# Another written-down order for the 5752 operations of a sparse-attention and two-layer mixture kernel

## The chip, the cores and the metric

The kernel runs on one core of a Trainium2 chip. The metric is the device time of one execution in microseconds; smaller is better. The time of the kernel before is the median of three runs.

## What is computed

Three stages follow each other (4 batches, 8 heads, 576 rows, head size 64; 2304 tokens of width 512; 8 experts with 1024 hidden units):

```python
scores = scale * np.matmul(q, k.transpose(0, 1, 3, 2))
kth = np.partition(scores, -32, axis=-1)[..., -32:-31]
scores = np.where(scores >= kth, scores, -1e9)          # the 32 largest of each row
attn = softmax(scores);  x = attn @ v                   # tokens, 8 heads side by side
logits = x @ w_gate + modality_bias[modality_id]
e = argmax(logits);  g = softmax(logits)[e]
x = g * (relu(x @ w1[e]) @ w2[e])                       # one expert for each token
h = x @ w_in;  solu = h * softmax(h)
out = layernorm(solu) * g_ln @ w_out
```

## The kernel before

**Attention.** The rows of a batch are cut into five tiles (four of 128 rows and one of 64). For each tile and pair of heads PE makes the scores (`pS`, L628). ACT copies them into `ss` (L649, L659), and DVE finds the 32nd largest value of each row: a maximum and a minimum of the two halves (L661, L662), then rounds of MAX8 and MATCH_REPLACE8 (L665 to L678). POOL and ACT make the masked exponentials `e` (L689 to L693). PE transposes them (L722, L733) and multiplies with the values (`po`, L755). ACT copies that into `oT` (L762), and one more matmul, `px` (L765), waits for the copy and gives the tile's rows and gate logits.

**Routing.** When the four pairs of a tile are done, its tokens are routed: DVE, POOL, ACT and PE work out the expert and the place of each token in that expert's list (the last step on DVE is L853, which adds to the count `cq`), and POOL scatters the rows into a list in DRAM (L858).

**First expert layer.** 14 slots of 128 tokens (`PLAN`) and a last, larger one take tokens from the lists. A slot may be taken when a given number of tokens is routed: 256 for slot 0, 384 for slot 1 and so on. POOL and DVE pick the fullest expert (L908, L915, L794 to L920), POOL gathers its rows from DRAM (`xg`, L933), PE transposes them (L960), DVE copies the result (`xT`, L966), and PE multiplies (`ph`, L1025; ACT makes `hh`, L1030; `py`, L1046). SP loads the expert's weights. The last slot uses fp32r matmuls of 448 columns (L1326, L1346) on split weights.

**Second layer.** Each group of 128 finished tokens goes through `moe2`: 24 matmuls of 512 columns into `u` in two halves (`ph`, L1067; ACT copy L1071; DVE maximum L1073, L1076; POOL L1077), exponentials on ACT (L1082), their product on DVE (L1084), the sums on POOL (L1090 to L1097), then two turns. A turn is four PE transposes of a half of `u` (L960), an ACT copy into the high part `lT` (L964), a DVE subtraction into the low part `lT` (L968) and 12 matmuls into `po` (L1128; the weights are `wo`). At the end ACT scales (L1137) and POOL scatters to the output (L1139).

Before all that, both second-layer weights are prepared from 64-bit floats (`statics`, L383 to L470) among the first attention tiles.

**The order.** The work is written as generators, called threads here (one for each unit of attention, pair, route, slot, group of tokens and so on). Each yields operations for one engine, or waits for buffers and events. At build time `Order.run` lists the threads that have an operation ready, and a digit of the table `ORDER` (base 36) says which one goes next:

```python
ready = [t for t in self.threads if t["op"] is not None]
...
if self.order is not None:
    th = ready[int(next(self.order), 36)]
...
op = th["op"]
op.fn()
```

So the table alone sets the sequence in which each engine's instructions stand, and which buffer each tile gets. Every engine runs its instructions in that sequence and waits where an operand isn't there yet. The costs that stand beside the operations are not used where a table is given, other than for bookkeeping.

Of the kernel before, what the change touches and what calls it, by code (L numbers as in the profile page):

```python
# [36 lines left out]
       "w": 4.587, "prep": -3.306, "ffn": 1.734, "front": -0.797, "static": -2.917, "const": -1.332}  # L37

ORDER = (
    "0022556001111111222202334444441115555513333554455556663666440000011233434366666667777555622223377703344441"  # L40
    "1225663226045437747747406244166644451000031111111130400000411333300033442121332155132333044345113544003002"
    "2221556420644464341444401111133622511114446463624461162233636556444412225115552666643315111111814443333332"
    "6675575751944228611434436633667114411111133011114445411122543323522224400445222255336065046005555110432222"
    "2200005561700205223616333333302660022221146007728584472226901553333384557744446661633334115665656213333547"
    "6222677788111425113316778122311145366676522233011100660001230005544112222222225113501133400555600511222467"
    "3311111115525444000113230000230550034434441111111000520002222113355555667335733302112446666553550000388877"
    "7617999894446361111118002455511220050005777444710005350053344992201187472242665111145333133311461114466115"
    "5115688888823662244166661743233223355443434343345352234452222622116010011224443304678776434234311224005511"
    "1112234343320335500044435553226610055671534444521053153536744154224526332222112002244003335255333000002344"
    "4611751160131557833333323436522245334775677676271166114492534763247788222283226233334623225577777766445443"  # L50
    "3666661226222757564126542524655772333043333115055353400042255000400223323000000011154021200042224004443456"
    "78822224811334555258570007301637788822662aa887800653347844785761334521604111100225562266644123333000046551"
    "1160011662242344552772060044034011120001112242112466666601177777665654522756565558856765888403033331133223"
    "2013232224445501133365533446553366001828333378835558803335454572201322621224411111455666163322412221154577"
    "2331301122305533334240113355541224551111110231200332456700543432224677757747418776662661777741365774422545"
    "3313436111022000133232455000111133335689842321434337422667533115511377122222254506411333453666112222245613"
    "4461556663347250132886868954424444442445663316666561111556111777745110433226565116231234002005555554331311"
    "1111144443152244533545545774201000122335444461551111322205300233400001331200134332400002211167880000544440"
    "2427351115453300000001022686622222474748807877112328664441140343345527704500442522666600077826558868990114"
    "5950411555700007556555034220222004455116665771581118882882223444445502266665773225100011111165335455522506"  # L60
    "0000022153231232311333466661102224255664134221115544432422233033555517757000102667788655522111115544127774"
    "4552311111000555777772944664304707225241115866282735311441434334455599033554aa445519a555775589633ab9255989"
    "8266400511166711167353011115001948882555007420344773333115766565576778945636776785157012334799993388942145"
    "5457443333233324656311022244222344003422300400011116614544336115844113393225957556641110500022272554440024"
    "6776225666200117734300100044846781711665333316744411411300172722999a64466977177763333311177859a11b11113354"
    "4488558188991116626227000555142553677677622264405245663362222554223633302220456666661145451111220885772655"
    "8776340846a91446767567755555552711111334455551288544122467133233035536531424250111111333465541100533222511"
    "4456063121332337891884545413355555254454622233622224775663557223337751130511689377454333512442266171455411"
    "22222005550000007654445577722802633725588a2bb01668888748717457559a6699973334556674445997a339a9aa9991155333"
    "3888888955674444555116877179444424541118167111304331221134434344555602344894331312334433455015556651566666"  # L70
    "4522222222215454666342111000231114444006006612301344220011661111104266726634311111311232555464113342884855"
    "56a430115881a811776533122252666645657528311899555583331332831466899998811188bb3377871178787111974553999799"
    "a91572722244469999a66333388544b559966136794444014367676226356566539181115555114377311117222992542433555446"
    "46467464647161333728111116633552223322776655645415111656578444017658744a9999132222244255568343322224445544"
    "47783333557672222111731223588667544224623389a6a886aa222755227898865534441111158944492557702264676387377765"
    "6558882993336646444064177166767014583376444499555779551878553555577a80999566673444628833333a69997aa4579944"
    "49778b8999925533a4444433000775507777755996663377433008341aaa1898805772434700003444356634444477760677800000"
    "2247744221111155566763333400200246611442200433333304001114110043400046631203446344644522115624545662226666"
    "656110441486697aa8779978873a444466448a22995588644409145801115701112700000441004661145511221333211222233332"
    "3351125555644025473222245733642236363677225453332272067751116575578888792222542422252078871668451133748666"  # L80
    "643345454564001544446000000333333565004460055788866777000706228389a965552336111155534113432351144302240556"
    "3333773331503400047776618902040655650053448827176368007883375345061111112224555444110344347227311111634322"
    "4306236676446386678344347572211666112244555677177845336655542222233554545318882456555824778355366623333356"
    "6255711422234462226760005006620400004754617322330072426665522222288226625000007464115566654005400040677666"
    "5787428000302221224453541110100223413344678777767711232222263450333555699772283455000000114356722355564343"
    "6011133711133322277111166661133266333366264511454545446222222266651444661342755227777733009586117344005451"
    "1332200000043345120522112216133114465667720221100411422222244553500012553232321243443445225331000000006767"
    "7734455454433554967757932233302271336655454666222788111133573454472215556660266699445323363332077472441314"
    "4455221113006622233600002364000023322246656557342220036433166222212000055005402004322444133233334230031300"
    "3330022222220002222202311121222341442220000000000221144000022110000000234444333333311331222533007700476666"  # L90
    "6666666444453455223333333111333323221115101111444223332202002200000111221100001111122324341132220022240002"
    "2444000000100133435523005004422121113345122111101230041443344030021100000000000000000000000000000011220000"
    "2221100001111111111111222222222230222331100022221113400300001222221100000002110000000000000011111000000001"
    "1111122033221000000000000000"
)
UNITS = 4
NEG = -3.0e38
# [1572 lines left out]
```

## Time and profile before

| | |
|---|---|
| median of 3 runs | 955.14 us (952.91 to 955.68) |
| profiled execution, its own time | 952.62 us |
| its span, first to last instruction | 950.8 us |
| PE busy | 874.6 us, 92% |
| DVE busy | 779.7 us, 82% |
| ACT busy | 670.9 us, 71% |
| POOL busy | 585.1 us, 62% |
| mean granted TensorE clock | 0.972 of full speed |

The span is 1.8 us shorter than the execution's own time. PE counts as busy while a matmul runs; PEld is its weight loads, which run beside matmuls. The windows view, quoted below, gives each engine's busy time in stretches of the span.

### The profile page before, as it was taken

To read this page: it belongs to the slowest core of one execution; us is meant where nothing else is said; L and a number is where in the kernel's file an instruction comes from. 1 tells how busy PE (TensorE), PEld (TensorE's weight loads), DVE (VectorE), ACT (ScalarE), POOL (GpSimd) and SP (SyncE) were. 2 spreads that over 40 slices of the span, in tenths; PEclk is the share of its full clock that TensorE was granted. 3 is DMA by queue.
4 is the path that set the end of the run, shared out by engine and by line. 5 is a ranking of instruction groups with operands and counts; after the bars stand their busy time and mean duration, and the time that the engine had idled before them with its cause. 6 is when DMAs were issued, how large, how long until landed. Compare 5 with 4: busy or idle time off the path is not lost.

```text
span 950.8 us, 21544 instructions
## 1 busy us (share of the span) xinstructions
PE 874.6 (92%) x6830; PEld 730.7 (77%) x6830; DVE 779.7 (82%) x2444; ACT 670.9 (71%) x1698; POOL 585.1 (62%) x1352
## 2 busy tenths in 40 slices
PE   5766787989999999999999999999999999999994
PEld 3544455977888888879888888888887988889872
DVE  7998998999999999999999999999999943422320
ACT  3867876878787778878877788788778863633432
POOL 4677856657666767675677677666677666520222
PEclk9888887999999999999999999999999999999998
DMA  6624233444624343455243434443432337624000
GB/s 173 188 67 138 91 89 93 124 115 140 174 79 148 112 137 113 119 157 154 79 137 103 125 90 138 121 123 113 136 96 86 114 107 224 195 89 118 6 23 26
DMA packets 140952, 110.72 MB, mean 116 GB/s; under 512 B 47233, under 2 KB 116893, under 8 KB 140830
## 3 DMA queue, kind: packets, MB, share of 16 engines
q1 hardware_dynamic: 136478, 93.92, 34.4%
q0 software_dynamic: 4352, 15.34, 4.7%
q8 instruction: 56, 0.92, 0.4%
q14 instruction: 66, 0.54, 0.2%
HBM read 97.11 MB, written 12.13 MB: 115 GB/s over the span
## 4 chain that ended last, share of the span: by engine, by line
PE 50%; DVE 14%; POOL 10%; ACT 5%; issue 5%; DMA 2%; POOLq 0%; DVEq 0%; ACTq 0%
PE po L1128 7%; PE ph L1025 7%; PE py L1046 7%; PE ph L1067 6%; PE po L755 5%; PE pS L628 4%; PE pt L722 4%; DVE M L669 3%; POOL e L691 2%; PE py L1346 2%; PE ph L1326 2%; DVE tht L678 2%; DMA xg<-xlist,li 2%; PE pt L960 1%; PE px L765 1%
## 5 line engine op out<-in xcount | busy, mean ns | idle before, releaser
L691 POOL TENSOR_TENSOR e<-ss,e 128x576 f32<-128x576 f32 x144 | 206.3, 1434 | 55.4 <-ACT e L690 52.9
L693 ACT ACTIVATE e<-e,nb 128x576 f32<-128x576 f32 x144 | 112.0, 778 | 25.7 <-POOL e L691 24.7
L669 DVE MATCH_REPLACE8 M<-tops,M 128x288 f32<-128x288 f32 x288 | 127.4, 445 | 0.0
L1025 PE MATMUL ph<-xT,wraw 128*128 128x128 f32 x960 | 126.2, 278 | 1.1 <-DVE M L662 0.5
L1046 PE MATMUL py<-hh,wraw 128*128 128x128 f32 x960 | 125.8, 278 | 1.1 <-ACT hh L1030 1.1
L690 ACT ACTIVATE e<-ss,bt 128x576 f32<-128x576 f32 x144 | 111.5, 778 | 19.4 <-POOL bt L689 19.2
L1025 PEld LDWEIGHTS ph<-xT,wraw 128*128 128x128 f32 x960 | 115.4, 192 | 6.3 <-issue 3.1
L1046 PEld LDWEIGHTS py<-hh,wraw 128*128 128x128 f32 x960 | 115.3, 192 | 5.6 <-issue 2.7
L1128 PE MATMUL po<-wo,lT 128*128 128x512 f32 x432 | 112.0, 404 | 2.6 <-ACT lT L964 2.6
L1067 PE MATMUL ph<-wi,yT 128*128 128x512 f32 x432 | 110.2, 403 | 0.8 <-ACT ss L649 0.7
L755 PE MATMUL po<-eT,vt 128*64 128x128 f32 (+1 forms) x1600 | 104.7, 273 | 5.2 <-DVE qT L533 1.9
L678 DVE MAX8 tht<-M 128x8 f32<-128x576 f32 x144 | 108.1, 754 | 1.2
L628 PE MATMUL pS<-kT,qT 64*128 64x288 f32 (+1 forms) x864 | 94.4, 322 | 10.0 <-DVE xs L776 4.3
L755 PEld LDWEIGHTS po<-eT,vt 128*64 128x64 f32 x1600 | 84.6, 140 | 20.7 <-ACT eT L725 5.8
L1128 PEld LDWEIGHTS po<-wo,lT 128*128 128x128 f32 x432 | 77.6, 188 | 23.8 <-DVE lT L968 3.3
L1067 PEld LDWEIGHTS ph<-wi,yT 128*128 128x128 f32 x432 | 78.3, 188 | 19.8 <-issue 1.6
L628 PEld LDWEIGHTS pS<-kT,qT 64*128 64x128 f32 (+1 forms) x864 | 72.2, 193 | 27.0 <-issue 7.8
L725 ACT ACTIVATE eT<-pt 128x512 f32<-128x512 f32 x144 | 82.0, 597 | 10.4 <-PE pt L722 9.8
L722 PE MATMUL pt<-identr,e 128*128 128x128 f32 x576 | 85.0, 284 | 4.1 <-ACT e L693 1.7
L722 PEld LDWEIGHTS pt<-identr,e 128*128 128x128 f32 x576 | 68.8, 146 | 12.7 <-ACT e L693 3.5
L661 DVE TENSOR_TENSOR M<-pS,ss 128x288 f32<-128x288 f32 x144 | 64.7, 450 | 9.3 <-ACT ss L659 7.2
L689 POOL TENSOR_SCALAR bt<-tht 128x1 f32<-128x1 f32 x144 | 34.0, 236 | 62.2 <-DVE tht L678 51.7
(256 smaller groups left out, 1848.4 us busy)
## 6 DMA issues: line engine op xcount, KB each, us to landing
wraw<-in_moe_w_dram SPq DMA_DIRECT2D x256, 256.0 KB
kr<-in_k_dram SPq DMA_DIRECT2D x32, 128.0 KB
qr<-in_q_dram SPq DMA_DIRECT2D x16, 256.0 KB
raw<-in_moe_w_out_dram SPq DMA_DIRECT2D x8, 512.0 KB
vt<-in_v_dram SPq DMA_DIRECT2D x32, 128.0 KB
raw<-in_moe_w_in_dram SPq DMA_DIRECT2D x8, 512.0 KB
wstage<-da SPq DMA_DIRECT2D x8, 256.0 KB
wc<-wstage SPq DMA_DIRECT2D x8, 256.0 KB
```

The costliest lines, as they stand in the source:

```text
L628: nc.tensor.matmul(bank[s][hf], x[r, a, p, :], kt[r, c, at:at + HALF], start=i == 0, stop=i == 2)
L669: nc.vector.match_replace(out=M, in_to_replace=rounds[r], in_values=M, imm_value=NEG)
L678: t0 = yield Op("DVE", 660, lambda: nc.vector.max(th, W), deps=[t0, tm])
L690: yield Op("ACT", 667, lambda: nc.scalar.activation(e, ss, AF.Relu, bias=bt, scale=-BIG))
L691: yield Op("POOL", 1360, lambda: nc.gpsimd.tensor_tensor(e, ss, e, op=OP.subtract))
L693: yield Op("ACT", 760, lambda: nc.scalar.activation(e, e, AF.Exp, bias=nb, scale=0.125, accum_out=z))
L722: nc.tensor.transpose(pt[:, c, :], ef[:, at:at + 128], ident)
L755: nc.tensor.matmul(po[hs, :n], w, x, start=c == 0, stop=c == 4)
L1025: nc.tensor.matmul(ph[:, :n], w[:, kk * 128:(kk + 1) * 128], x[0][:, kk, :n], start=kk == 0, stop=kk == KD - 1)
L1046: nc.tensor.matmul(py[c // k_][:, c % k_, :], w[:, c * 128:(c + 1) * 128], hs[m], start=m == 0 and c % k_ == 0, stop=m == KF - 1 and c % k ...
L1067: nc.tensor.matmul(ph, y[a][:, kk, :], wi[b][:, kk, i * 512:(i + 1) * 512], start=kk == 0 and j == 0, stop=kk == KD - 1 and j == 2)
L1128: nc.tensor.matmul(po, l[a][:, c, :], wo[b][:, kk, :], start=kk == 0 and j == 0, stop=kk == KF - 1 and j == 2)
```

## The change

Only the table `ORDER` is another one. Both tables have 5752 digits; the first 11 are the same, and 4864 of all differ. The operations, their shapes, the buffers' numbers and the plan of slots are the same.

```diff
 ORDER = (
-    "0022556001111111222202334444341111115555513333554455556663666440000011233434366666667777555622223377703344441"
...
+    "0022556001101111220112334441144455551445446666556657427747773222333327775335888447777436655355541288886662"
...
 )
```

**The last matmuls on PE.** Two groups of tokens are the last to go through the second layer. Here `po_14028` and `po_14112` are their results before, `po_14017` and `po_14090` after; `po_13894` is the result of the group ahead of them. A row of `L960` with `u` is a turn's transposes. Before:

```order
L1067 MATMUL ph<-wi_98,yT 128x512
L960 MATMUL pt<-identr,u 128x128 x4
L1128 MATMUL po_14028<-wo_100,lT 128x512
...
L960 MATMUL pt<-identr,u 128x128 x8
L1128 MATMUL po_14028<-wo_100,lT 128x512
...
L1128 MATMUL po_14112<-wo_100,lT 128x512
...
L960 MATMUL pt<-identr,u 128x128 x4
L1128 MATMUL po_14112<-wo_100,lT 128x512
```

Now:

```order
L1128 MATMUL po_13894<-wo_100,lT 128x512
...
L960 MATMUL pt<-identr,u 128x128 x4
L1128 MATMUL po_13894<-wo_101,lT 128x512
...
L1128 MATMUL po_14017<-wo_100,lT 128x512
...
L960 MATMUL pt<-identr,u 128x128 x8
L1128 MATMUL po_14090<-wo_100,lT 128x512
...
L960 MATMUL pt<-identr,u 128x128 x4
L1128 MATMUL po_14017<-wo_100,lT 128x512
...
L1128 MATMUL po_14090<-wo_100,lT 128x512
```

Behind the last L1067 stand 48 matmuls of L1128 before, and 60 now: 12 of the group ahead moved behind it, six on either side of the first turn's transposes. The two last groups now take turns, so that between the last transposes and the matmuls which read them stand 12 of the other group.

**The second route on DVE.** These are DVE's rows around the last step of the second tile's routing (L853) up to the pick's first step (L915); the other rows are attention units, the weights' low parts (`wo`) and the low parts of `qT`. Before:

```order
L669 MATCH_REPLACE M<-tops,M 128x288
L851 TENSOR_TENSOR rk<-pc,cq 128x8
L852 SCALAR_TENSOR_TENSOR rk,pos<-rk,oh 128x8
L853 TENSOR_TENSOR cq<-cq,pc 128x8
L665 MAX tops<-M 128x8
L672 MAX tops<-M 128x8
L669 MATCH_REPLACE M<-tops,M 128x288
L470 TENSOR_TENSOR wo_101<-pw,wo_100 128x512 x2
```

Now:

```order
L470 TENSOR_TENSOR wo_101<-pw,wo_100 128x512
L669 MATCH_REPLACE M<-tops,M 128x288
L533 TENSOR_TENSOR qT<-pt,qT 64x4x64
L851 TENSOR_TENSOR rk<-pc,cq 128x8
L852 SCALAR_TENSOR_TENSOR rk,pos<-rk,oh 128x8
L853 TENSOR_TENSOR cq<-cq,pc 128x8
L672 MAX abt<-M 128x8
L533 TENSOR_TENSOR qT<-pt,qT 64x4x64
```

DVE now has 299 instructions up to and with this L853 in place of 293, and in both orders 338 up to and with the first copy of gathered rows (L966). So 39 stand from the route to the copy in place of 45.

## Rows read from the trace of the kernel before

**Rows 1.** The page's part 1: busy time, share of the span, instructions.

```profile
PE 874.6 (92%) x6830; PEld 730.7 (77%) x6830; DVE 779.7 (82%) x2444; ACT 670.9 (71%) x1698; POOL 585.1 (62%) x1352
```

**Rows 2.** Windows: us, then busy time of each engine, granted clock, DMA share, GB/s.

```profile
0.00:10.00 10.00, 4.41 (x22) 3.20 (x22) 4.25 (x17) 3.66 (x8) 1.96 (x15) 1.00 0.45 96
10.00:165.00 155.00, 114.15 (x620) 71.92 (x622) 144.91 (x394) 110.53 (x259) 109.39 (x164) 0.86 0.41 123
165.00:200.00 35.00, 34.45 (x323) 31.83 (x322) 34.73 (x117) 28.27 (x78) 22.86 (x55) 1.00 0.42 123
200.00:750.00 550.00, 537.30 (x4710) 465.50 (x4709) 523.72 (x1710) 439.04 (x1149) 372.29 (x915) 1.00 0.42 122
750.00:900.00 150.00, 148.40 (x1004) 131.18 (x1003) 61.02 (x187) 73.54 (x182) 64.02 (x168) 1.00 0.40 123
900.00:950.80 50.80, 35.84 (x159) 27.10 (x157) 11.06 (x23) 15.86 (x29) 14.57 (x38) 0.91 0.06 23
```

**Rows 3.** PE's timeline at the end: start, us, instructions, idle before and its releaser.

```profile
915.35 5.75 PE L1067 MATMUL ph<-wi,yT 128*128 128x512 f32 x24
921.85 0.66 PE L960 MATMUL pt<-identr,u 128*128 128x128 f32 x4 [0.75 <-DVE u L1084]
923.20 3.32 PE L1128 MATMUL po<-wo,lT 128*128 128x512 f32 x12 [0.69 <-ACT lT L964]
926.36 1.03 PE L960 MATMUL pt<-identr,u 128*128 128x128 f32 x8
928.60 6.13 PE L1128 MATMUL po<-wo,lT 128*128 128x512 f32 x24 [1.21 <-ACT lT L964]
934.56 0.60 PE L960 MATMUL pt<-identr,u 128*128 128x128 f32 x4
935.85 3.33 PE L1128 MATMUL po<-wo,lT 128*128 128x512 f32 x12 [0.69 <-ACT lT L964]
```

**Rows 4.** Timelines of ACT and DVE in the same stretch.

```profile
918.34 0.60 ACT L1071 ACTIVATE u<-ph 128x512 f32<-128x512 f32 x1 [1.54 <-PE ph L1067]
921.10 0.69 DVE L1084 SCALAR_TENSOR_TENSOR u<-u,ex 128x512 f32<-128x512 f32 x1 [1.25 <-ACT ex L1082]
939.30 0.69 ACT L1137 ACTIVATE ot<-po,hrs 128x512 f32<-128x512 f32 x1 [3.50 <-PE po L1128]
```

**Rows 5.** Whom PE waited for, from 10 to 165 us: total, times, longest.

```profile
PE px L765 <- ACT oT L762: 6.8, 3, 3.6
```

**Rows 6.** DVE's groups, 10 to 165 us: busy, mean ns, idle before, releaser.

```profile
L661 DVE TENSOR_TENSOR M<-pS,ss 128x288 f32<-128x288 f32 x26 | 11.7, 449 | 4.0 <-ACT ss L659 3.6
```

**Rows 7.** Timelines of DVE, POOL and PE from the second route to slot 0.

```profile
146.97 0.15 DVE L853 TENSOR_TENSOR cq<-cq,pc 128x8 f32<-128x8 f32 x1
158.62 1.10 POOL L933 DMA_INDIRECT xg<-xlist,li  x1 [0.29 <-POOL li L929]
164.28 0.63 PE L960 MATMUL pt<-identr,xg 128*128 128x128 f32 x4 [0.18 <-DMA xg<-xlist,li]
165.34 0.68 DVE L966 COPY xT<-pt 128x512 f32<-128x512 f32 x1
```

**Rows 8.** The tile `xg`, all gathers: landing after issue, and who waited for it.

```profile
DMA to landing us min/median/max: 3.5/4.5/6.3
DVE xT L966: 2.4, 2
```

**Rows 9.** Whom PE waited for, 200 to 905 us: total, times, longest; the longest row.

```profile
PE px L765 <- ACT oT L762: 2.6, 4, 1.4
```

More of the change, by code (lines that the diff above doesn't have):

```diff
@@ L45 @@
[L45 to L54, printed above, removed]
@@ new lines @@
+    "2233223377544545420880112434236636663555662111122220111115455512445515551511211444454422222112223333666113"
+    "3677784664844663352111111114453311466771167444662422235434533444363637777333312222234322221144466551518833"
+    "4435355339777288224444113324677688511211211155334446665565666222372233333113333445655777771161168722024833"
+    "364422764382847945557586992411222555222a4488333989442aa292277444a33335563351353366887025343333211555467771"
+    "8331873333226226676888853113114444112222551114666566788437777221214222352111138335117133335562222688137331"
@@ new lines @@
+    "1122666223222222235112441111112255451611114334444444133111111666656a147372244aa3a3677774455556119427135517"
+    "7761261369999787111173632227776224251111133888171113445356658591113713163122241322220112222243111364111555"
+    "5111156776334777754544116666657333522253254343442133244452226222233441611554545451145762678742523411524162"
+    "22222225514322324455555555133155404551451162351344434336201166666773113222204472226565568117772222027a6644"
+    "2266464472211535668637322022222226234211516656511613540701811001175772221192999991335336676626241121334343"
@@ new lines @@
+    "3422555576337144457752056556777776215277441122834266512111342551133443434111111321155111222312444312444689"
+    "aa2333029166334862388066005582200012aaa0777bb8998934541622627600052200011131722264677550113332300005665771"
+    "1170031302720170043355600466411520041444300222668822888899999882484113267676788595956678666666925441122656"
+    "5651777834222574441772263345689181074232222220673604122673357761573325887774644455712263522222222664541341"
+    "1045414324420011144552254555514660021440013400000024234556745440055522115552561878733155684688777751336544"
@@ new lines @@
+    "5522223362222205541140343146455552226111731022557441213374221168484911556614642265506443433375366777121111"
+    "533706773363254599899a689548155555524459476611342216655611177671835511677634226577117786311153888645222222"
+    "7771222233662545456605571436222443151232342444666511500012000440000313112111343433671170010055667322114331"
+    "1363465555221111455220630073322228265511576466723111112603666353357006664700007700729944477777833a66688289"
+    "0116a1119187115166734448376675373887777333833a122456647838833266776765567837833468512131331225837225554312"
@@ new lines @@
+    "8011202544504355355302277788226646344878976772222222331099482615452333043334466610030778151121467633320077"
+    "7000003700555555666111661615657776300662449983332347756264545456668999a3033745564541133688784444699aa84781"
+    "032284813361447676111114611868841110100915546644444488129878a77899896b7579467a8877122553999aaa892258444708"
+    "45444333333126634452122553347773116433316611142222885344366112995522833b4477366622211544112322285673558511"
+    "63633737112288887452220221166555562278855073355536111711460111aaa452289a88582123aabb498999aa40330330244496"
@@ new lines @@
+    "98a64001988a5511614744832110155578828474643998754087785533446633633226233620666666462231777177220776267884"
+    "4348446940178787878666666789785261511884412377779974664537725512274646464677447367776122451172444562222213"
+    "1225568816667421477776565657112322146554253325466222246225776345520223257717554223777754662253345563333342"
+    "08227851115111066114456608000077777211265627589aa0155a9966185556667493355689994533444744444588337798996998"
+    "9851155767678885588894411941545584422333663336222111153353114113354553652834547778223455456331677727777565"
@@ new lines @@
+    "6333332333365646666778722224111551122442551771134552423112222222373773354445892288777722222238444b37757527"
+    "ab77771115325aa5888892472231118378838808794946466522988328482414663899988881121442997265651165651133344116"
+    "25777777786746966a45579aaaabb744668747454442554918847833367676035669999777a1255115344931111222228868296353"
+    "6456464664377311855255511552222122111534347766266115653678722465657752222544666256533011449352448433326467"
+    "451573334457577162222533112266885272433689aa89956555222267679222788887393312242222131816766333478877775650"
@@ new lines @@
+    "254477757875753aa788328807553a91455826333388036733305422224263315653368888365557247333357722222599889634b3"
+    "999222558789bb000755877333333888377088255558366a43333994660019a9a80733440000030444335664438744337766777000"
+    "0042211138885555116166111333510000220511666221454444161157703633333464111166666576335782446651621173633625"
+    "5053446016577644449359a50446757776133336643346637332783311557544440066650074330000436626667722774665543442"
+    "2503433847777455277131111115662255346424336225643377205677116614589777888262222277163111006667334665755462"
@@ L95 @@
+    "6666663333316334755001553444444435000551172233366222010204331133333302222220000111002222322322320033300246"
+    "6611100011101103345522100222311131231112233443311102001000332222333002000000000001000000000000002330002223"
+    "3222222330223314334443221143333221122452400220110000000000303011112210003301101111111111112222201110021120"
+    "1111110302211110022110100000"
 )
```

55 lines of the change are left out of this document (10 added, 45 removed).

## Prediction

> **What bounds the kernel now.** I read the busy shares first, then the stretches, then the timeline of the end, and last the place where the first expert slot starts. PE is busy 92% of the span and DVE 82% [rows 1], but these are averages over stretches with different limits [rows 2]. From 10 to 165 us DVE is busy 144.91 of 155.00 us and PE only 114.15: there is no expert work yet, so attention on DVE sets the pace, and DVE's 10.1 us of idle time are what an order could win there. From 200 to 750 us PE is busy 537.30 of 550.00 us and DVE 523.72, and from 750 to 900 us PE 148.40 of 150.00. So behind slot 0's start PE is the bound, with 12.7 and 1.6 us of idle time in those two stretches. In the last 50.80 us PE works 35.84 us: there it waits on its own last results.
>
> The end is the plainest part [rows 3]. The last L1067 is over at 915.35 + 5.75 = 921.10 us and the last L1128 at 935.85 + 3.33 = 939.18, so this tail takes 18.08 us. The work in it is 48 matmuls of L1128 at 5.75 / 24 = 0.240 us (the row of 24 back to back) = 11.5 us, and 16 transposes in 0.60 + 1.03 + 0.60 = 2.2 us: 13.7 us. The other 4.35 us are gaps: each turn's transposes or matmuls wait for DVE or ACT with nothing put between, and the first L1128 of a turn run stretched (3.32 us for 12 in place of 2.88) while the low part is still being made.
>
> **The change, part by part.** It adds and removes no instruction: DVE has 338 up to the first gathered copy in both orders, and the diff touches the table alone. So busy time should stay, and all that can change is who waits.
>
> *The tail.* Behind the last L1067 stand 60 matmuls now: 60 x 0.240 = 14.4 us, with transposes 16.6. Which gaps stay? The first group's second half of L1067 now ends 12 matmuls (2.88 us) before the last L1067 does. From the ACT copy of such a half to the transposes of its turn took 921.85 - 918.34 = 3.5 us [rows 3, 4], so those are ready some 0.7 us after the last L1067, and six matmuls of the group ahead (1.4 us) stand in that place: covered. Its eviction (the 0.69 us gap and the stretched start, together about 1.1 us) is covered by the other six. The eight transposes in the middle evict with nothing but the second four between: I leave half of 1.1 us there, 0.6, where the row before shows 1.21 because ACT was busy. The last turn is covered by 12 matmuls of the other group. So the tail is 16.6 + 0.6 = 17.2 us, and it holds 12 matmuls (2.88 us) that stood ahead before, where PE had no gap: the gain is 18.08 + 2.88 - 17.2 = 3.8 us. Bounds: 4.35 if no gap stays; 2.6 if the middle gap stays whole (1.21 + 0.5). What comes after PE, from the ACT scale at 939.30 us to the span's end, 11.5 us [rows 4], is the same.
>
> *Up to slot 0.* In these 155 us PE stood 6.8 us in three waits of `px` for the ACT copy `oT` [rows 5]. Behind `px` in PE's order stand the next scores, and DVE's L661, which needs their copy, sat idle 4.0 us [rows 6]. Counting PE's instructions between a pair's last `po` and its `px`: of the ten pairs ahead of the first expert matmul, three had none before (the first, fourth and tenth), and one has none now (the seventh); the second to fourth now have 12 or 13. So I expect about half of L661's 4.0 us back, 2.0 us. Bounds: all of DVE's 10.1 us, and a loss from the gather below.
>
> *The gather of slot 0.* From the second route to the copy of slot 0's rows DVE took 165.34 - 146.97 = 18.4 us for 45 instructions, 0.41 us each, and PE's wait for the rows was 0.18 us [rows 7], so the gather was just hidden. Now 39 instructions stand there: 6 x 0.41 = 2.5 us less cover. Behind the waiting copy the whole attention on DVE is queued, and behind PE's transposes the next `po`. But the six instructions are not lost, they stand ahead of the route, and POOL's list between scatter and gather (L858 to L933) is as long as before. I take no loss: the route's own steps (L851 to L853) had idle time in front of them which now has work in it. Bound: 2.5 us.
>
> *The middle.* Other waits of PE are short and many; the longest, `px` for `oT`, is 2.6 us in four waits [rows 9]. Of the 70 pairs behind the first ten, `px` directly behind its `po` stands twice before and twice now. I take 0; bounds are a gain of all 14.3 us of PE's idle time, and a loss from later slots: the DVE instructions from route to copy fall from 48 to 44 at slot 1, 50 to 45 at slot 5 and 55 to 47 at slot 6, and rise or stay within three at slots 2, 3, 4 and 7. At 0.41 us those are 1.6, 2.0 and 3.3 us of cover.
>
> *Sum.* 3.8 + 2.0 = 5.8 us. The profiled execution (952.62) would take 946.8; it lies 2.5 us under the median of 955.14. Against the median: 955.14 - 5.8 = **949.3 us**.
>
> **Rivals.**
>
> A. *The middle closes up too.* If the new order spares half of the middle's 14.3 us (7.1), the time is 949.3 - 7.1 = 942.2. For it speaks that DVE has 26.3 us of idle time from 200 to 750 us, so it could follow; against it, that the waits there are scattered and the counts above don't change. Chance 0.14.
>
> B. *The gather of slot 0 shows.* The head's 2.0 us don't come and 2.5 us of stall come in their place: 955.14 - 3.8 + 2.5 = 953.8, within the measurement. For it: only 0.18 us of slack in the rows; against it, as argued, that DVE's queue ahead has more work in it. Chance 0.17.
>
> C. *Slower: several gathers are uncovered.* Slots 0, 1, 5 and 6 lost 2.5, 1.6, 2.0 and 3.3 us of cover, 9.4 us together. A stall at L966 holds every attention unit behind it, and the later routes with them. If all show and only the tail's 3.8 us come back: 955.14 - 3.8 + 9.4 = 960.7. It decides for slower once 6.7 us show (3.8 plus 0.3% of the time). Against it: in all 14 gathers L966 waited 2.4 us on two occasions only [rows 8], and gathers land 3.5 to 6.3 us after issue, so most had slack. Chance 0.10.
>
> D. *PE isn't full in the middle.* The matmul row says 537.30 of 550.00 us, the weight-load row 465.50 [rows 2]. If the 537 were waits drawn out as work, DVE would be the next limit and its 26.3 us could go: 949.3 - 26.3 = 923.0. By the row of 24 matmuls in 5.75 us, which had no idle time before it and none inside, I hold PE's busy time for real work and give this 0.02. The Trainium skill ("Perfetto Trace Analysis", Identifying the Most-Contended Engine) says that matmul busy share is no good measure of how near TensorE is to its limit, and that the share of weight loads is; by that rule the middle would have 15% in hand. No run here shows that yet.
>
> That the table is the same program in effect isn't a rival: 4864 digits differ, and the sequences of all five engines do.
>
> **How the numbers follow.** The forecast has 0.57; its own range, from the tail's and head's bounds, is 945 to 952.5. Runs of this kernel scatter by about 0.3% (2.9 us), which I take as what can be told from no change: faster means under 952.3. The forecast is there with nearly all its chance; with A and D that is 0.69 after a little for the forecast's upper edge. Same, B and that edge: 0.19. Slower, C and a smaller share of B with worse luck: 0.12. The range of 8 in 10 reaches from A's 942 down to 941.5, and up to 957, part of the way to C.
>
> **What would show it.** *Right:* the stretch from the last L1067 to the last L1128 is about 17.2 us long with 60 matmuls, and L1128 waits for `lT` at most once there; `px` waits for `oT` less than 4 us in the head; slot 0's copy L966 starts near 163 us; PE's busy time stays within 3 us of 874.6. *Wrong:* L966 or L960 waits for gathered rows by over 2 us at slots 0, 1, 5 or 6; slot 0 starts after 165.3 us; PE's idle time from 200 to 900 us differs from 14.3 us by more than 4.

## The result and the profile after

| | before | changed |
|---|---|---|
| median of the runs | 955.0 us (952.91 to 955.68, 4 runs) | 941.82 us (940.89 to 944.39, 4 runs) |
| ratio | | 0.987 [0.9845, 0.9895] |
| profiled execution, its own time | 952.62 us | 944.39 us |
| its span | 950.8 us | 942.5 us |

The change makes the kernel faster by 13.2 us. The forecast was a gain of 5.8 us, so more than half of what came isn't in its sum. The profiled execution of the changed kernel is the longest of its four; another profiled one (below, the full change again) took 941.35 us.

Busy times of the changed kernel, as [rows 1]:

```profile
PE 874.3 (93%) x6830; PEld 729.7 (77%) x6830; DVE 773.9 (82%) x2444; ACT 670.3 (71%) x1698; POOL 582.4 (62%) x1352
```

PE's busy time is the same to 0.3 us in these two profiles (874.6 before; the changed kernel's second profile has 870.7). So nearly all of the time between the two comes out of waits. Where, the windows of the changed kernel tell, beside [rows 2]:

```profile
0.00:10.00 10.00, 4.41 (x22) 3.19 (x22) 4.17 (x17) 3.63 (x8) 1.96 (x15) 1.00 0.45 99
10.00:165.00 155.00, 115.86 (x613) 71.02 (x614) 143.73 (x391) 109.22 (x255) 108.01 (x160) 0.83 0.41 121
165.00:200.00 35.00, 35.00 (x323) 32.15 (x322) 33.50 (x116) 27.05 (x76) 21.96 (x55) 0.98 0.47 136
200.00:750.00 550.00, 540.49 (x4738) 467.67 (x4738) 524.46 (x1724) 444.90 (x1163) 375.60 (x921) 1.00 0.42 122
750.00:900.00 150.00, 148.85 (x1010) 132.33 (x1005) 59.09 (x179) 71.79 (x175) 63.71 (x174) 1.00 0.40 121
900.00:942.50 42.50, 29.66 (x136) 23.32 (x134) 9.01 (x19) 13.66 (x25) 11.21 (x28) 0.90 0.07 27
```

Up to 165 us nothing is won in this execution: DVE has 391 instructions behind it where it had 394. From 200 to 900 us PE's idle time is 9.51 + 1.15 = 10.7 us instead of 14.3, and the last window begins with less work left: 136 matmuls instead of 159.

PE's timeline at the end of the changed kernel, as [rows 3]:

```profile
904.85 8.56 PE L1067 MATMUL ph<-wi,yT 128*128 128x512 f32 x36
913.25 1.56 PE L1128 MATMUL po<-wo,lT 128*128 128x512 f32 x6
914.65 0.60 PE L960 MATMUL pt<-identr,u 128*128 128x128 f32 x4
915.00 4.44 PE L1128 MATMUL po<-wo,lT 128*128 128x512 f32 x18
919.28 1.03 PE L960 MATMUL pt<-identr,u 128*128 128x128 f32 x8
920.56 3.33 PE L1128 MATMUL po<-wo,lT 128*128 128x512 f32 x12 [0.25 <-ACT lT L964]
923.73 0.60 PE L960 MATMUL pt<-identr,u 128*128 128x128 f32 x4
924.08 5.83 PE L1128 MATMUL po<-wo,lT 128*128 128x512 f32 x24
```

From the last L1067 (904.85 + 8.56 = 913.41) to the last L1128 (924.08 + 5.83 = 929.91) it is 16.5 us with 60 matmuls of L1128, where it was 18.1 us with 48. Of the four gaps of [rows 3] (0.75, 0.69, 1.21 and 0.69 us) one of 0.25 us is left.

Whom PE waited for between 10 and 165 us, the rows that answer to [rows 5] (one wait of `px` is put down to L690), and DVE's L661 there, as [rows 6]:

```profile
PE px L765 <- ACT e L690: 4.6, 1, 4.6
PE px L765 <- ACT oT L762: 2.2, 2, 1.6
```

```profile
L661 DVE TENSOR_TENSOR M<-pS,ss 128x288 f32<-128x288 f32 x25 | 11.2, 448 | 4.9 <-ACT ss L659 4.4
```

`px` waits 4.6 + 2.2 = 6.8 us in three waits, to the tenth what it was, and L661 sat idle 4.9 us instead of 4.0. Slot 0's copy (timelines of POOL and DVE, as [rows 7]) and all gathers (as [rows 8]):

```profile
159.65 1.09 POOL L933 DMA_INDIRECT xg<-xlist,li  x1 [0.29 <-POOL li L929]
166.38 0.69 DVE L966 COPY xT<-pt 128x512 f32<-128x512 f32 x1 [0.34 <-PE pt L960]
```

```profile
DMA to landing us min/median/max: 3.5/4.7/5.6
  DVE xT L966: 2.1, 3
```

The gather starts 1.0 us later than before and the copy too; DVE waits 0.34 us. Over all slots L966 waits 2.1 us in three waits, before it was 2.4 in two. PE's transposes wait once for gathered rows, 0.8 us at slot 2 (246 us); no other gather came to light.

The middle, 200 to 870 us (up to about the last slot's L1346), in one window; first the kernel before, then the changed one:

```profile
200.00:870.00 670.00, 655.69 (x5523) 569.74 (x5522) 574.87 (x1868) 499.76 (x1289) 431.93 (x1067) 1.00 0.43 126
```

```profile
200.00:870.00 670.00, 659.34 (x5556) 573.58 (x5555) 572.48 (x1873) 502.52 (x1297) 431.84 (x1070) 1.00 0.43 126
```

PE idles 10.7 us instead of 14.3 and does 33 matmuls more in the same time. The longest of its waits there, before and then after:

```profile
PE px L765 <- ACT oT L762: 2.6, 4, 1.4
PE pc L844 <- POOL oh L839: 2.1, 3, 1.2
PE pt L960 <- ACT eT L725: 1.5, 1, 1.5
PE py L1046 <- ACT hh L1030: 1.1, 2, 0.6
PE pt L733 <- ACT eT L725: 1.0, 2, 0.5
```

```profile
PE px L765 <- ACT oT L762: 1.9, 3, 1.1
PE po L755 <- ACT eT L725: 1.4, 3, 0.7
PE pt L722 <- DVE rz L707: 1.0, 1, 1.0
PE pt L722 <- ACT e L693: 1.0, 2, 0.6
PE pc L844 <- POOL oh L839: 1.0, 1, 1.0
```

No wait stands out in either: before there are 26 of 0.2 to 1.5 us, after 18 of up to 1.1, and mostly others. The idle time of the middle scatters too: with the tail alone new (below) it is 16.2 us in the old order, with the new middle it is 9.0 to 10.7 us in six profiles.

Waits are not all of it. PE's largest group of scores in the same window, before and after, is the same 576 matmuls:

```profile
L628 PE MATMUL pS<-kT,qT 64*128 64x288 f32 x576 | 53.7, 311 | 0.3 <-ACT xs L771 0.2
```

```profile
L628 PE MATMUL pS<-kT,qT 64*128 64x288 f32 x576 | 52.4, 310 | 0.3 <-DVE M L662 0.3
```

PE is busy with them for 1.3 us less, and so it is in all six profiles with the new middle (52.4 us; 53.6 or 53.7 in four with the old one).

### The profile page after: what moved, and what is told of

It is laid out like the page before. It is cut to its first block, busy times and chain, and to the rows that moved or that the text cites. A ratio compares the mean times of both kernels' runs of the same rounds, so it can differ in the third digit from the quotient of the medians.

```text
span 942.5 us, 21521 instructions
## 1 busy us (share of the span) xinstructions
PE 874.3 (93%) x6830; PEld 729.7 (77%) x6830; DVE 773.9 (82%) x2444; ACT 670.3 (71%) x1698; POOL 582.4 (62%) x1352
## 4 chain that ended last, share of the span: by engine, by line
PE 64%; DVE 11%; POOL 6%; ACT 5%; issue 3%; DMA 1%; POOLq 0%; DVEq 0%; ACTq 0%
PE ph L1025 10%; PE ph L1067 9%; PE py L1046 9%; PE po L1128 8%; PE po L755 6%; PE pS L628 5%; PE pt L722 5%; DVE M L669 2%; PE py L1346 2%; PE ph L1326 2%; POOL e L691 2%; PE px L765 2%; PE pt L960 2%; PE pw L408 2%; DVE tht L678 1%
## 5 line engine op out<-in xcount | busy, mean ns | idle before, releaser
L691 POOL TENSOR_TENSOR e<-ss,e 128x576 f32<-128x576 f32 x144 | 204.7, 1423 | 55.6 <-ACT e L690 54.1
L690 ACT ACTIVATE e<-ss,bt 128x576 f32<-128x576 f32 x144 | 111.1, 776 | 14.6 <-POOL bt L689 14.3
L1128 PE MATMUL po<-wo,lT 128*128 128x512 f32 x432 | 112.3, 405 | 0.5 <-DVE lT L968 0.2
L1067 PE MATMUL ph<-wi,yT 128*128 128x512 f32 x432 | 109.7, 402 | 0.0
L628 PE MATMUL pS<-kT,qT 64*128 64x288 f32 (+1 forms) x864 | 91.5, 324 | 3.9 <-DVE M L662 2.8
L725 ACT ACTIVATE eT<-pt 128x512 f32<-128x512 f32 x144 | 82.4, 598 | 15.7 <-PE pt L722 14.9
L1128 PEld LDWEIGHTS po<-wo,lT 128*128 128x128 f32 x432 | 77.5, 188 | 20.7 <-DVE lT L968 3.4
L1067 PEld LDWEIGHTS ph<-wi,yT 128*128 128x128 f32 x432 | 78.5, 188 | 18.2 <-issue 1.2
L628 PEld LDWEIGHTS pS<-kT,qT 64*128 64x128 f32 (+1 forms) x864 | 71.6, 197 | 20.7 <-issue 8.8
L649 ACT ACTIVATE ss<-pS 128x288 f32<-128x288 f32 x144 | 58.0, 411 | 22.1 <-PE pS L628 15.1
L661 DVE TENSOR_TENSOR M<-pS,ss 128x288 f32<-128x288 f32 x144 | 64.9, 451 | 9.9 <-ACT ss L659 7.7
```

The source lines that it names most:

```text
L628: nc.tensor.matmul(bank[s][hf], x[r, a, p, :], kt[r, c, at:at + HALF], start=i == 0, stop=i == 2)
L690: yield Op("ACT", 667, lambda: nc.scalar.activation(e, ss, AF.Relu, bias=bt, scale=-BIG))
L691: yield Op("POOL", 1360, lambda: nc.gpsimd.tensor_tensor(e, ss, e, op=OP.subtract))
L1067: nc.tensor.matmul(ph, y[a][:, kk, :], wi[b][:, kk, i * 512:(i + 1) * 512], start=kk == 0 and j == 0, stop=kk == KD - 1 and j == 2)
L1128: nc.tensor.matmul(po, l[a][:, c, :], wo[b][:, kk, :], start=kk == 0 and j == 0, stop=kk == KF - 1 and j == 2)
```

## The experiments

**How a part was changed alone.** The first runs join the two orders at a point in time: the first N operations stand in the one order, all others in the sequence that they have in the other. Landmarks are operation 930 (933 in the new order), slot 0's first expert matmul at some 166 us; 3165 (3170), the end of a route at some 511 us; and 5576 (5578), the last slot's L1346 at some 870 us. In the code each is another table `ORDER` and nothing else. So the runs are old/new in four pieces: head, first part of the middle, second part, tail.

**PE's distance.** The executions differ by several us in the head alone, so beside the medians I use a distance: when PE has done the same matmul work, less that time in the profile of the kernel before. Work is the sum of the matmuls, each line's at its mean time in the rows at full clock; it is good to some 0.5 to 1 us. The last column is the end of the last L1128, read off directly.

| PE's distance (us) | at 200 | 510 | 690 | 870 | PE's end |
|---|---|---|---|---|---|
| changed kernel | +1.4 | +0.3 | -2.5 | -4.5 | -9.3 |
| the same again | -0.6 | -2.7 | -5.3 | -7.2 | -12.0 |
| old head, rest new | +2.0 | -0.6 | -3.4 | -5.6 | -10.5 |
| middle alone new | +3.6 | +1.7 | -1.6 | -3.9 | -2.4 |
| tail alone new | +0.6 | +2.6 | +2.5 | +2.3 | -2.6 |
| three single moves | +0.6 | +1.9 | +1.8 | +1.9 | +2.1 |

### The tail alone

```diff
-    "2444000000100133435523005004422121113345122111101230041443344030021100000000000000000000000000000011220000"
+    "2444000000100133435523005004422121113345122111101230041443344030100202000000000001000000000000002330002223"
...
```

> The order of before up to the end of the last slot's L1326 and L1346 (5576 of 5752 operations), the new order for the rest. Theory T (the gain lies in the tail, as the forecast had it, and what is over 3.8 us is there too): 942 to 945 us. Theory S (the gain is spread: about 4.5 us in the tail, the rest in the stretches ahead of it): 950 to 951 us, and in its profile the last L1128 ends about 16.5 us after the last L1067.

Measured: 949.32 us against 954.34, ratio 0.9944 [0.9926, 0.9961], a gain of 5.0 us. The stretch from the last L1067 to the last L1128 is 16.5 us, the same as in the full change. By the distance the tail wins 4.9 us here (+2.3 to -2.6), 4.8 in the full change.

### The head alone

```diff
-ORDER: operations 1 to 933 in the old sequence
+ORDER: operations 1 to 933 in the new sequence, all others in the old one
```

> The new order up to the first expert matmul (933 operations, 166 us in the profile of before), the order of before for the rest. Theory H (the head gives what the forecast gave it, 2 us, or more): 950 to 953 us. Rival G (the head loses, since slot 0's rows come later: its copy L966 started 1.0 us later in the one profile of the change): 955 to 958 us.

Measured: 952.7 us against 954.34, ratio 0.9977 [0.9963, 0.9991]: 1.6 us. But the rows that the forecast built on didn't move. `px` waits for `oT` 7.2 us in four waits between 10 and 165 us, and L661's idle time is 5.3 us. In ten profiles with the old head `px` waits 6.8 to 7.4 us and L661 idles 2.4 to 4.6, in six with the new one 6.8 to 8.2 (with the wait that is put down to L690) and 3.9 to 5.3. From 200 to 870 us, where the order is the old one, PE idles 12.4 us in this run's profile, against 14.3 in the kernel before and 16.2 with the tail alone new. So the 1.6 us may be won behind the head; one profile doesn't show it.

### The first half and the second half

```diff
-ORDER: all operations in the old sequence
+ORDER: operations 1 to 3170 in the new sequence, the others in the old one
...
+ORDER: operations 1 to 3165 in the old sequence, the others in the new one
```

> The new order up to the end of the eleventh tile's route (3170 operations, about 511 us), the order of before for the rest. Theory S with the stretches as the two profiles show them (behind by about 3 us at 510 us): 956 to 959 us. If the first half has a gain that the one profile of the change did not show: 948 to 952 us.

> The order of before up to the end of the eleventh tile's route (3165 operations), the new order for the rest. Theory S: the tail's 4.5 us and 5 to 6 us from 511 us to 870 us, so 944 to 946 us, and with the first half's loss gone perhaps less than the changed kernel's 941.8. Theory T: 942 to 951 us with nothing in the stretch from 511 to 870 us.

Measured: the first half 951.02 us, ratio 0.997 [0.9953, 0.9987], 3.3 us; the second half 947.95, ratio 0.9932 [0.9914, 0.995], 6.4 us. The second half gives more than the tail's 5.0, but the two halves together make 9.7 of the 13.2, so the sum alone settled nothing.

### The full change again, without its tail, and without its head

```diff
-ORDER: all operations in the new sequence
+ORDER: operations 1 to 5578 in the new sequence, the others in the old one
...
+ORDER: operations 1 to 930 in the old sequence, the others in the new one
```

> The changed kernel once more, as it is, beside the two below and with more runs. If its 13.2 us were partly scatter of few runs and the pieces add up (first half 3.3, second half 6.4): 944 to 946 us. If the pieces gain by being together: 941 to 943 us.

> The new order up to the end of the last slot's L1326 and L1346, the order of before for the tail. If the tail's 5.0 us (as alone) simply add to the rest: 5 us over the changed kernel's time of the same call, 946 to 950 us. If the new tail needs the new order ahead of it: 7 us or more over it.

> The order of before up to the first expert matmul, the new order for the rest. If the head's 1.6 us (as alone) simply add: 1 to 3 us over the changed kernel of the same call. If the head's gain is an illusion of scatter: the same as the changed kernel within 1 us.

Measured, against 955.07: the full change 941.73, ratio 0.9873 [0.9841, 0.9905]; without its tail 948.95, ratio 0.9938 [0.992, 0.9955], 6.1 us; without its head 942.56, ratio 0.9873 [0.9839, 0.9906], 12.5 us. So 6.1 us are there with the old tail and 12.5 with the old head: something between the two gives most of what the forecast missed.

### The middle alone, and its two parts

```diff
-ORDER: all operations in the old sequence
+ORDER: operations 931 to 5578 in the new sequence, those before and behind in the old one
...
+ORDER: from 931 to 3170 alone in the new sequence
...
+ORDER: from 3166 to 5578 alone in the new sequence
```

> The old order up to slot 0's first expert matmul (first 930 operations), the new one until the last slot's L1346 is through (operation 5578), the old one in the tail: head and tail are the old ones, the middle alone is new. Theory M (the step 'the middle, I take 0' failed: most of PE's scattered waits between slot 0 and the last expert slot went): the middle gives 5.9 to 7.6 us, the distance that PE gained between 200 and 870 us in the four profiles of the full change, of the change without its tail and without its head; so 947.5 to 949.5, ratio about 0.9935, and PE's idle time between 200 and 870 us near 9 us instead of 14. Rival S (the parts only work together: head, tail and middle each give little alone, the full 13.3 us needs all): 952 to 954. Rival 0 (the forecast as it was): 955.

> The old order up to slot 0's first expert matmul, the new one until the end of route 11 (about 511 us), then the old one: the part of the middle from 166 to 511 us alone. Theory M: 1.7 us of the middle's gain lie here by the profiles (PE's distance to the kernel before grew from +0.8 to -0.9 us in the run of the first half, from -0.6 to -2.3 in the full change), so about 953.5, ratio 0.998. Rival S or 0: 955.

> The old order up to the end of route 11 (operation 3165, about 511 us), the new one until the last slot's L1346 is through, the old one in the tail: the part of the middle from 511 to 870 us alone. Theory M: 4.5 to 5.1 us (PE's distance grew by 5.1 us there in the run of the second half, by 4.9 in the full change), so about 950, ratio 0.995. Rival S or 0: 954 to 955. The two parts' gains should add up to that of the middle alone.

Measured, against 955.63: the middle alone 948.5, ratio 0.9924 [0.9903, 0.9945], 7.1 us; its first part 951.4, ratio 0.9962 [0.9946, 0.9978], 4.2 us; its second part 952.29, ratio 0.9969 [0.9955, 0.9982], 3.3 us. The window 200 to 870 us of the middle alone:

```profile
200.00:870.00 670.00, 660.55 (x5564) 574.58 (x5563) 573.52 (x1877) 504.20 (x1302) 433.38 (x1077) 1.00 0.43 127
```

PE idles 9.5 us there (670.00 - 660.55) in place of 14.3. Theory M holds as to the place of the gain, rival S and the forecast's 0 fall. Cut in time at these points, the pieces add up: head 1.6, middle 7.1, tail 5.0 make 13.7, the whole 13.2. The cut into halves made 9.7; with intervals of 3 to 6 us in width the two sums can't be told apart. The split between the two parts is another than I expected (4.2 and 3.3 for 1.7 and 4.5 to 5.1), and both expectations lie just outside the intervals (2.1 to 5.2 and 1.7 to 4.3). In the profiles of these two runs PE's distance falls by some 1.5 us in the first part and some 5 us in the second, as expected. Which of the two splits is right stays open.

### Single moves at single waits

If PE sets the pace, a wait taken away should be won. Three moves in the old order, at its three longest waits of the middle; the third is seen in the timelines of ACT and POOL of the kernel before:

```profile
713.43 0.78 ACT L690 ACTIVATE e<-ss,bt 128x576 f32<-128x576 f32 x1 [2.05 <-POOL bt L689]
714.11 1.07 ACT L725 ACTIVATE eT<-pt 128x512 f32<-128x512 f32 x2
```

```profile
711.45 1.10 POOL L933 DMA_INDIRECT xg<-xlist,li  x1 [0.52 <-POOL li L929]
712.63 0.77 POOL L689 TENSOR_SCALAR bt<-tht 128x1 f32<-128x1 f32 x1
```

ACT stood still 2.05 us in front of L690, which needs POOL's L689, which stood behind a gather's issue; the copies L725, for which PE waited, stood behind L690.

```diff
 ACT, at 212 us
+L762 ACTIVATE oT<-po 128x128
 L649 ACTIVATE ss<-pS 128x288
 L1082 ACTIVATE ex,hse<-u,hnm,gate 128x512
-L762 ACTIVATE oT<-po 128x128
 PE, at 477 us
-L844 MATMUL pc<-oh,tri 128x8
-L845 MATMUL pc<-oh,ones 128x8
 L1128 MATMUL po_7327<-wo_100,lT 128x512
+L844 MATMUL pc<-oh,tri 128x8
+L845 MATMUL pc<-oh,ones 128x8
 ACT, at 714 us
-L690 ACTIVATE e<-ss,bt 128x576
 L725 ACTIVATE eT<-pt 128x512 x2
 L740 ACTIVATE eT<-pt 128x128
+L690 ACTIVATE e<-ss,bt 128x576
```

With the second move DVE's L851 to L853, which follow on PE's L844, also go behind two attention instructions that stood after them.

> The old order with three single moves at its three longest PE waits in the middle, nothing else: (1) at 212 us ACT's copy oT (L762) goes ahead of the L649 and L1082 it stood behind, PE waited 1.37 us there; (2) at 477 us PE's L844 (with DVE's L851 to L853) goes behind the six L1128 that follow it, PE waited 1.21 us for oh there; (3) at 714 us ACT's three copies eT (L725, L740) go ahead of L690, which kept ACT waiting for POOL, PE waited 1.49 us there. Theory M (PE sets the pace in the middle, so each wait taken away counts whole and doesn't come back): the waits become about 0.5, 0 and 0.4, together 3.2 us less; in the profile PE's distance to the kernel before falls by about 0.9 at 212, 1.2 at 477 and 1.1 at 714 and stays there until 870; time about 951.8, ratio 0.9967. Rival G (what is saved at one wait is given back at the next, since DVE, ACT or POOL are as full): the distance is back to where it was within 50 us of each move, time 955.

Measured: 955.45 us against 954.36, ratio 1.0013 [0.9997, 1.0029]: nothing. PE's timeline of the kernel before at the three places, and right behind the first and the third:

```profile
212.13 0.51 PE L765 MATMUL px<-iw,oT 128*128 128x144 f32 x2 [1.37 <-ACT oT L762]
223.66 0.66 PE L722 MATMUL pt<-identr,e 128*128 128x128 f32 x4 [0.53 <-ACT e L709]
477.09 0.17 PE L844 MATMUL pc<-oh,tri 128*128 128x8 bf16 x1 [1.21 <-POOL oh L839]
714.74 0.66 PE L960 MATMUL pt<-identr,u 128*128 128x128 f32 x4 [1.49 <-ACT eT L725]
716.57 0.66 PE L960 MATMUL pt<-identr,xg 128*128 128x128 f32 x4
```

and of the kernel with the three moves:

```profile
212.86 0.51 PE L765 MATMUL px<-iw,oT 128*128 128x144 f32 x2 [0.37 <-ACT oT L762]
225.82 0.66 PE L722 MATMUL pt<-identr,e 128*128 128x128 f32 x4 [1.20 <-ACT e L709]
479.07 2.05 PE L1128 MATMUL po<-wo,lT 128*128 128x512 f32 x6 [0.69 <-ACT lT L964]
715.43 0.66 PE L960 MATMUL pt<-identr,u 128*128 128x128 f32 x4
718.08 0.66 PE L960 MATMUL pt<-identr,xg 128*128 128x128 f32 x4 [0.75 <-DMA xg<-xlist,li]
```

All three waits went as meant: 1.37 to 0.37, 1.21 to none, 1.49 to none. In their place PE waits for something else: 13 us behind the first for `e`, 1.20 us where it was 0.53; at the second 0.69 for `lT`; 2 us behind the third 0.75 for gathered rows. From 510 to 870 us the distance is 0.4 to 0.7 us smaller than in the run with the new tail, which has the old order there without the moves. Rival G holds nearly whole, and theory M falls in the form "each wait counts". So the run of the middle alone shows where the gain is, and which of its many moves make it stays open.

### The new order with two single moves

```diff
 PE, at 322 us
-L844 MATMUL pc<-oh,tri 128x8
-L845 MATMUL pc<-oh,ones 128x8
 L1046 MATMUL py<-hh,wraw 128x128 x8
+L844 MATMUL pc<-oh,tri 128x8
+L845 MATMUL pc<-oh,ones 128x8
 POOL, at 481 us
-L1139 DMA_INDIRECT out_dram<-ot,oid
...
 L691 TENSOR_TENSOR e<-ss,e 128x576
+L1139 DMA_INDIRECT out_dram<-ot,oid
```

With the first move DVE's L851 to L853 also go behind one attention instruction that stood after them.

> The new order with two single moves at PE waits of the middle that it still has: at 322 us PE's L844 goes behind the eight L1046 that follow it (PE waited 0.96 us for oh), at 481 us POOL's scatter L1139 goes behind the L691 that waits behind it (PE waited 0.76 us at the end of that chain). Theory M: 1.7 us less than the changed kernel, so about 940.1, ratio 0.9853. Rival G: 941.7, as the changed kernel. The medians alone can hardly tell these two apart; the two waits in the profile can.

Measured: 943.38 us against 954.36, ratio 0.9875 [0.9854, 0.9895]: as the changed kernel. Against the changed kernel's second profile the two waits went (0.96 to none, 0.76 to 0.35), and at the next ones PE waits 0.67 us for 0.31 and 1.05 for 0.57. The medians can hardly tell 1.7 us; the waits speak for rival G again.

### Interleaving and inner order apart

The new middle differs from the old in how expert work and attention alternate, and in the order inside each. Each half alone:

```diff
-ORDER: operations 931 to 5578 in the new sequence
+ORDER: the same places for attention and for experts as in the new sequence, each class in its old inner order
...
+ORDER: the same places as in the old sequence, each class in its new inner order
```

Where an operation would stand ahead of what it needs, it follows as soon as that is there, so a small part of the places (a tenth at most) are other ones.

> The middle alone (operations 931 to 5578), and of its new order one half: where an operation of attention (its units, pairs, routes and loads) and where one of the expert slots and the second layer stands is as in the new order, but the operations of each of the two classes keep the old order among themselves. Head and tail are the old ones. Theory I (the gain of the middle, 7.1 us, lies in how the two classes are interleaved: what PE has to do for the experts stands where attention makes it wait): about 949, ratio 0.993, PE idle near 9.5 us from 200 to 870 us. Theory O (it lies in the order inside the classes, which attention unit's step comes first): 954 to 956. Theory W (it is neither alone; only the two together fit): 953 or more here and in the other run, slower too, since the halves don't match.

> The other half: the operations of attention among themselves, and those of the experts and the second layer among themselves, stand in the new order, but the places of the two classes alternate as in the old one. Head and tail are the old ones. Theory I: 954 to 956. Theory O: about 949, ratio 0.993. Theory W: 953 or more.

Measured: 1071.98 us, ratio 1.1233 [1.1207, 1.1259], and 1076.74 us, ratio 1.1291 [1.1263, 1.1318]. Theory W holds, far beyond what I had written. The window 200 to 750 us of the first of them, and PE's longest sorts of wait from 200 to 1000 us:

```profile
200.00:750.00 550.00, 485.80 (x3986) 407.96 (x3986) 450.28 (x1451) 372.77 (x976) 311.20 (x782) 0.97 0.37 106
```

```profile
PE px L765 <- ACT oT L762: 14.7, 19, 1.8
PE po L755 <- ACT eT L725: 7.8, 8, 4.2
PE pc L844 <- POOL oh L839: 7.7, 5, 2.7
```

and the window of the second:

```profile
200.00:750.00 550.00, 481.54 (x3924) 405.25 (x3923) 437.54 (x1416) 363.77 (x956) 308.20 (x768) 0.95 0.36 103
```

Against 4710 matmuls in 537.30 us [rows 2] there are 3986 and 3924, and every engine is less busy than before: PE by 52 and 56 us, DVE by 73 and 86. The granted clock is lower as well, 0.97 and 0.95 where it was 1.00. No engine is the bound in these two. All wait for each other, mostly at the same places as before but many times more, and some waits are long: up to 8.4 us in the second run.

## Why the prediction was wrong, point by point

**The middle: the step that failed.** It says "I take 0", with a bound of 14.3 us. The middle gives 7.1 us alone [0.9903, 0.9945], and 5.9 to 7.6 us by the distance between 200 and 870 us in four profiles. PE's idle time there fell by 3.6 to 5.3 us in them. Of the rest, some 2 us, 1.3 us are the shorter busy time of L628; why it is shorter, no run shows. The forecast had counted PE's own list (how often `px` stands right behind its `po`) and DVE's from route to copy. But the rows show waits whose cause stands in ACT's or POOL's list (`oT` behind L1082, `eT` behind a waiting L690, `oh` behind L691). Counts in one engine's list said nothing of those, so 0 was no finding but the lack of one. That these three sorts of wait make the gain isn't shown either: taken away in one place each they gave nothing.

**Rival A**, the middle closing by half of PE's idle time, gave 942.2 us and was nearest to the 941.8 measured. It got 0.14 because "the waits there are scattered and the counts above don't change". Both are true, and neither speaks against a gain, since the new middle won on scattered waits. That the number fits so well is luck in part: the tail gave 1.2 us more than in A's sum and the head 0.4 less. The forecast's own range, 945 to 952.5, doesn't follow from the bounds that it names: 4.35 and 10.1 us would give 940.7 at one end, 2.6 us less the gather's 2.5 would give 955.0 at the other.

**The tail** was right in its mechanism, and too small. Expected were 17.2 us with 60 matmuls, measured 16.5; `lT` is waited for once, 0.25 us where 0.6 was left for it. With 18.08 + 2.88 - 16.5 that makes 4.5 us by the rows against 3.8, a little over the bound of 4.35; the distance says 4.9 and the medians of the tail alone 5.0. In the full change the medians say 948.95 - 941.73 = 7.2 us, with intervals of 3 and 6 us in width, and the distance 4.8. Part of this has a place: behind the new middle the old tail loses 1.5 us of distance (-3.9 to -2.4). Of these, 0.6 us lie behind the last L1067: 18.65 us in place of 18.08. PE's timeline there with the middle alone new, and the window of that row:

```profile
920.19 4.87 PE L1128 MATMUL po<-wo,lT 128*128 128x512 f32 x12 [0.69 <-ACT lT L964]
```

```profile
920.19:925.06 4.87, 4.87 (x14) 3.57 (x15) 2.07 (x7) 3.04 (x6) 4.03 (x13) 0.65 0.00 0
```

The 12 matmuls that took 3.32 us [rows 3] at a granted clock of 1.00 take 4.87 us at 0.65, and the wait behind them shrinks from 1.21 to 0.25 us. The stretch is 18.7 us long in five of the ten profiles with the old tail, the one of the head alone among them, and 18.1 in the others. So this isn't the new middle's doing.

**What comes after PE** was taken as the same, and isn't. POOL's timeline at the last scatter, before and after:

```profile
940.26 0.97 POOL L1139 DMA_INDIRECT out_dram<-ot,lx  x1 [6.12 <-ACT ot L1137]
```

```profile
932.05 0.97 POOL L1139 DMA_INDIRECT out_dram<-ot,lx  x1 [2.73 <-DMA out_dram<-ot,lx]
```

The last two groups now end close together, and the last scatter waits, by its row, for the one ahead to land. It starts 1.1 to 1.6 us after the end of the last L1137 in all six profiles with the new tail, and 0.3 us after it in all ten with the old one. From the start of that L1137 to the span's end it is 12.5 us here where it was 11.5 (12.2 to 12.8 in the six, 11.5 to 12.5 in the ten). So about 1 us of what the tail wins on PE is given back.

**Up to slot 0** 2.0 us were expected and 1.6 came, 0.8 by the run without the head. The size is about right and the reason isn't: `px` waits as long as before, and L661 idles no less. The condition "`px` less than 4 us" failed in all six profiles with the new head. What gives the 1.6 us, and whether it is won in the head at all, stays open.

**The gather of slot 0** costs next to nothing, as taken: DVE waits at its copy for 0.7 us at most in six profiles with the new head. Whether L966 comes near 163 us can't be told by one run: it starts at 163.06 to 168.61 us in ten profiles with the old head, at 163.85 to 166.38 in six with the new one.

**Rivals B and C** fell with it: L966 waits 2.1 us in all over the changed kernel's run, 1.4 at most at once. With 39 in place of 45 DVE instructions the cover was still long enough. A gather that no rival named does show: at slot 2 PE waits 0.8 to 1.4 us for rows in all five profiles with the new head and the new first part.

**Rival D** stays undecided as to its rule. PE's matmul row went up to 659.34 of 670.00 us, the weight-load row from 569.74 to 573.58; a drop of 26 us is in no run. That the middle has 15% in hand by the weight loads, as the rule of the Trainium skill ("Perfetto Trace Analysis", Identifying the Most-Contended Engine) would have it, no run here shows. But the single moves show that PE's high matmul share isn't a bound by itself either: three waits taken away gave 0.7 us at most of the 1.00 + 1.21 + 1.49 = 3.7.

**PE's idle time 200 to 900 us**, named as a sign that would show the forecast wrong if it moved by more than 4, went from 14.3 to 10.7 in the first profile and 10.1 in the second: just at that limit, with a gain of 6 us behind it. It was too coarse a sign: the window stands still while the work moves through it.

## What to carry to other kernels

When a whole order is replaced by a searched one, "scattered short waits" are where the gain can lie: bound it by the idle time of the fullest engine in that stretch, and don't take 0; here about half of it came. Look for the cause of each wait in the list of the engine that is waited for, what stands ahead of the releaser there, and not in the list of the one that waits. Cut such a change in time to find where its gain is: pieces along time add up here to within their intervals, while single moves give nothing, and one order's interleaving with the other's inner order costs 12%. And look past the fullest engine at the end: what it wins can be lost in part to the last transfers.

## What was not expected of the chip

Executions of the same instructions differ in the head by several us. In ten profiles the first 930 operations stand in the old order, and slot 0's copy begins between 163.06 and 168.61 us; the granted clock from 10 to 165 us is 0.82 to 0.86 in them, without a plain relation to the time (0.83 with 164.26, 0.82 with 166.99, 0.84 with 168.61). Behind it an execution can keep what it has: with the tail alone new the distance stays between 2.1 and 2.7 us from 250 to 750 us. With the head alone new the distance falls by some 2 us in the middle, though the order there is the old one. Which event of the head makes the difference wasn't tried.

At all five places where a single move took a wait of PE away, more than a third of it was back within 15 us as a wait for another engine or a DMA, with PE at 98% by the matmul row (655.69 of 670.00 us): that row alone didn't tell that the next releaser was nearly as late.
